# Attention and gated-MLP backward on one core: dK and dV matmuls levelled over the halves of a head, projections spread, copies moved to ScalarE

## Chip, cores and metric

The kernel runs on one core of a Trainium2 chip. The metric is device time in microseconds of one execution, the median over runs. Engines are named as the profile names them: PE (TensorE matmuls), PEld (its weight loads), DVE (VectorE), ACT (ScalarE), POOL (GpSimd), SP (the queue that issues transposing DMAs here).

## The reference

The output and eight gradients of `x + s * silu(B(xn))` are computed, where `xn` is a layer norm of `x`, `s` is an attention block over a given K and V cache, and `B` a gated MLP. Sizes: 2048 tokens, model width 576, 32 heads of width 128, MLP width 4608, bf16.

```python
def _A_ref(x, k_cache, v_cache, wq, wo):            # per head, Dh = 128
    q = (x @ wq).reshape(B, Sq, H, Dh).transpose(0, 2, 1, 3)
    scores = jnp.einsum("bhqd,bhkd->bhqk", q, k_cache) * (Dh ** -0.5)
    p = _softmax(scores, axis=-1)
    o = jnp.einsum("bhqk,bhkd->bhqd", p, v_cache)
    return o.transpose(0, 2, 1, 3).reshape(B, Sq, H * Dh) @ wo
...
_out, _vjp = jax.vjp(_f, A_x, A_k_cache, A_v_cache, A_wq, A_wo, B_w_gate, B_w_up, B_w_down)
return (_out, *_vjp(grad_out))
```

For each head the backward pass needs P = softmax(Q K^T), O = P V, dV = P^T dO, dP = dO V^T, dS = P * (dP - delta) with delta the row sums of O * dO, dQ = dS K and dK = dS^T Q.

## The kernel before

The program has stages one after the other: the MLP forward, a small stage for `silu` and the gradient that enters the attention, then the 32 heads, then the output projection and the gradients of the weights and of `x`. Only the heads are touched here; they take about 470 to 3600 us of the span, and a few microseconds of tail.

**A head.** There are 16 q tiles of 128 rows (`NT`), and each is done in two halves of 1024 key columns. In the first phase `s_half` makes scores: two matmuls of 512 columns into a PSUM tile `sp` (pool `ps_big`, two buffers), then DVE writes `sneg` with a running minimum. `s_exp` on ACT makes `P` of the whole row of 2048 in one instruction, into a slab. In the second phase `dp_half` makes dP in the same two PSUM buffers; either ACT (with the bias `negdelta`, into `t`) and then DVE's multiplication, or DVE alone in one `scalar_tensor_tensor`, makes `dS`, into a slab too. For the q tiles in `STT2` (4, 9, 14) both halves go to DVE alone; for the others the first half goes by ACT. The pool `slab` has 20 buffers for the 16 `P` and 16 `dS` of a head.

O and dQ need `P` and `dS` transposed: `trans_dma` issues a transposing DMA from SP for each row (tiles `PT`, `dST`, 7 buffers); only `dS` of q tile 9 is transposed by TensorE (`PE_DS`, `trans_pe`). `row_mm` then accumulates four q tiles per PSUM bank (`rows`, 16 matmuls of 128 columns per tile), and `o_sink` or `dq_sink` takes the bank. dV and dK need no transpose: `kv_mm` takes 128 x 128 blocks of a slab as weights and accumulates over all 16 q tiles. One call of `kv` makes half of dV or of dK in two banks, with 128 matmuls ordered by q tile, eight for each; its `sink` copies the banks on ACT (`KVE`) and stores them. There are four such calls per head: VA and VB for dV, KA and KB for dK.

Beside these, per head: `prep_wo` transposes a block of Wo, `proj` makes Q^T (for the next head) and dO^T in four chunks of 512 columns with five matmuls each, and `prep_kt`, `prep_vt`, `prep_don`, `prep_qn` transpose K, V, dO^T and Q^T on TensorE, eight blocks per PSUM bank, two banks each, and copy them out. Pool scales dO (`s_scale`) and Q (`prep_qn`) by the softmax's factors. All of these take their PSUM banks from `ps_acc`, four buffers, which `row_mm` and `kv_mm` use too.

**What sets the order.** For PE, DVE and ACT the order of instructions is the order in which they are emitted (`manual_schedule(engines=MAN)`); Pool and SP are ordered by the framework. Every step is entered with a position: `anchor` for the 64 halves of a head (position = half, `s_half` 0 to 31, `dp_half` 32 to 63), `at` for all others. They are sorted by position, and each step is emitted behind the anchors up to its own position. A position is therefore a place between two halves, not a time. Work of a head may lie past 64, which is inside the next head. Before, a call of `kv` spread its 128 matmuls evenly from one position to another:

```python
VA, VB, KA, KB = (22, 38.0), (38.5, 53.5), (58.0, 69.5), (70.5, 82.0)
QP, DO, KVE, PJE, OUE = (41.0, 3.0), (4.0, 2.5), "ss", "sv", "s"
KT_AT, DON_AT, VT_AT, QN_AT = (46.3, 2, "v"), (7.2, 5, "v"), (22.2, 2, "v"), (38.3, 2, "s")
EXP_AT, RINV_AT, PT_AT, DST_AT, AFTER = 2.1, 4.6, 2.7, 2.0, 3.5
...
at(pos + (end - pos) * (qt * n + j) / (NT * n), kv_mm, bx, hs, slabs, rhs, half, qt, j, sink)
```

The letters choose the engine of a copy: "s" is ACT, "v" is DVE. `rows` of P V start at half 12.1 and of dS K at 44.1 (`XO`, `XQ`), two halves per q tile.

Of the kernel before, what the change touches and what calls it, by code (L numbers as in the profile page):

```python
# [95 lines left out]
def kernel(  # L96
# [312 lines left out]
    with tc.tile_pool(name="ld2", bufs=2) as ld2, tc.tile_pool(name="ld1q", bufs=1) as ld1q, \  # L409
# [17 lines left out]
        def at(pos, fn, *args):  # L427
            prog.append((pos, len(prog), fn, args))
# [56 lines left out]
            alt.copy(hs.woT[:, :DL, :], pt[:, :DL, :], eng=eng)  # L485
            alt.copy(hs.woT[P - KL:, DL, :], pt[P - KL:, DL, :], eng=eng)

        def proj(hs, name, c, eng):
            if c == 0:
# [6 lines left out]
            nc.tensor.matmul(acc[:], lhsT=w[:, DL, :], rhs=xnT[:, DL, cs], start=False, stop=True)
# [23 lines left out]
        def prep_qn(hs, g, eng):  # L520
            if g == 0:
                hs.Qn = ld1q.tile([P, NT, P], bf, name="Qn")
                nc.gpsimd.tensor_scalar(hs.rsc[:], hs.rinv_all[:], SCALE, None, op0=ALU.mult)
            pe_transposes(lambda j: hs.QT[:, j * P:(j + 1) * P], hs.Qn, g, eng)
            gs = slice(g * 8, (g + 1) * 8)
            nc.gpsimd.tensor_tensor(hs.Qn[:, gs, :], hs.Qn[:, gs, :], bcast(hs.rsc[:, gs], 8), op=ALU.mult)
# [142 lines left out]
        VA, VB, KA, KB = (22, 38.0), (38.5, 53.5), (58.0, 69.5), (70.5, 82.0)
        QP, DO, KVE, PJE, OUE = (41.0, 3.0), (4.0, 2.5), "ss", "sv", "s"  # L670
        KT_AT, DON_AT, VT_AT, QN_AT = (46.3, 2, "v"), (7.2, 5, "v"), (22.2, 2, "v"), (38.3, 2, "s")
        EXP_AT, RINV_AT, PT_AT, DST_AT, AFTER = 2.1, 4.6, 2.7, 2.0, 3.5
        WO_AT = 50.0
        MAN = {mybir.EngineType.PE, mybir.EngineType.DVE, mybir.EngineType.Activation}
        for h in range(H):
            hs = Head(h)
# [4 lines left out]
            for c in range(NCH):
                at(back(QP[0] + QP[1] * c), proj, hs, "QT", c, PJE[0])
                at(b + DO[0] + DO[1] * c, proj, hs, "dOT", c, PJE[1])
            at(b + DO[0] - 2, prep_wo, hs, "s")
            for g in range(2):
                at(back(KT_AT[0] + KT_AT[1] * g), prep_kt, hs, g, KT_AT[2])
                at(b + DON_AT[0] + DON_AT[1] * g, prep_don, hs, g, DON_AT[2])
                at(b + VT_AT[0] + VT_AT[1] * g, prep_vt, hs, g, VT_AT[2])
                at(b + QN_AT[0] + QN_AT[1] * g, prep_qn, hs, g, QN_AT[2])
            for p in range(NT // 2):  # L690
                at(b + 4 * p + 2 + RINV_AT, s_rinv, hs, p)
                at(b + max(4 * p + 2.1 + RINV_AT, DON_AT[0] + DON_AT[1] * (p // 4) + 0.5), s_scale, hs, p)
            for qt in range(NT):
# [4 lines left out]
                at(p1 + EXP_AT, s_exp, hs, qt)
                if qt in PE_P:
                    for g in range(2):  # L700
                        at(p1 + 5.3 + g, trans_pe, hs.PT, hs.P, qt, "PT", g, "s")
                else:
                    at(p1 + PT_AT, trans_dma, hs.PT, hs.P, qt, "PT")
                if qt in PE_DS:
                    for g in range(2):
                        at(p2 + 4.3 + g, trans_pe, hs.dST, hs.dS, qt, "dST", g, "sv"[g])
                else:
                    at(p2 + DST_AT, trans_dma, hs.dST, hs.dS, qt, "dST")
            for g in range(NG):
                rows(b + 8 * g + XO, 2, 2, hs, hs.PT, "Vn", g, o_sink(hs, g))  # L710
                rows(b + H1 + 8 * g + XQ, 2, 2, hs, hs.dST, "Kn", g, dq_sink(hs, g))
            for half, (pv, pk_) in enumerate(((VA, KA), (VB, KB))):
                kv(b + pv[0], b + pv[1], hs, hs.P, "dOn", half, out_3[0, h])
                kv(b + pk_[0], b + pk_[1], hs, hs.dS, "Qn", half, out_2[0, h])
# [350 lines left out]
```

## Time and profile before

| | us |
|---|---|
| median of 3 runs (lowest, highest) | 5124.49 (5123.4, 5145.9) |
| span of the profiled execution, first to last instruction | 5130.2 |
| time of the profiled execution itself | not given apart |
| busy: PE, PEld | 4970.7, 3593.9 |
| busy: DVE, ACT, POOL | 3252.2, 2268.8, 1473.0 |
| mean granted TensorE clock | 0.996 |

The profile lists the instructions of one execution by engine. A group is named by its line, engine and operation, the tile it writes and the tiles it reads. The end of a matmul is modelled (a matmul of 128 columns is given 219 ns although the next can start 56 ns after it), so times between starts are the better measure on PE. A wait of an engine is put down to the instruction that released the semaphore last.

### The profile page before, as it was taken

The numbers are of one execution on the slowest core, as the hardware profiler recorded it, in microseconds if no ns is written. First come the engines' busy times: TensorE is split into PE (matmuls) and PEld (weight loads), VectorE is DVE, ScalarE is ACT, GpSimd is POOL, SyncE is SP. The second block draws the span as 40 slices with busy tenths as digits, with TensorE's granted clock in tenths as the row PEclk, the third lists the DMA queues.
The fourth block names the chain that finished last, engine by engine and source line by source line (L and its number), as shares of the span: only waits on it lengthen the run. The fifth ranks groups of instructions, "written<-read, shape, count | busy, mean of one in ns | idle before, by whom it ended". The sixth has DMA issues, their size and how long they took to land.

```text
span 5130.2 us, 127328 instructions
## 1 busy us (share of the span) xinstructions
PE 4970.7 (97%) x54403; PEld 3593.9 (70%) x55312; DVE 3252.2 (63%) x5077; ACT 2268.8 (44%) x2875; POOL 1473.0 (29%) x2165
## 2 busy tenths in 40 slices
PE   9998999999999999999999999999899999999999
PEld 3344777777777777777777777777757777754554
DVE  6546888888888888888888888878633222210101
ACT  5523655655665566556556655655402222100000
POOL 4322323332333233223323332332222333211000
PEclk9999999999999999999999999999999999999999
DMA  7886999999999999999999999999998776697775
GB/s 261 266 216 153 193 198 201 194 199 199 195 193 200 199 193 201 199 196 197 194 202 198 199 199 199 190 188 198 208 200 240 205 202 192 207 244 158 154 153 119
DMA packets 2712809, 1013.48 MB, mean 198 GB/s; under 512 B 2525744, under 2 KB 2648624, under 8 KB 2712240
## 3 DMA queue, kind: packets, MB, share of 16 engines
q1 hardware_dynamic: 2626976, 719.49, 81.3%
q0 software_dynamic: 85264, 285.79, 19.1%
q8 instruction: 432, 7.08, 0.6%
q14 instruction: 137, 1.12, 0.1%
HBM read 172.54 MB, written 201.00 MB: 73 GB/s over the span
## 4 chain that ended last, share of the span: by engine, by line
PE 84%; DVE 6%; issue 5%; DMA 4%; POOL 1%; SPq 1%; ACT 0%; DVEq 0%; POOLq 0%; ACTq 0%
PE acckv L615 17%; PE acc L596 15%; PE acc L1006 8%; PE dp L566 7%; PE sp L536 5%; PE accw L888 5%; PE accp L495 5%; DVE sneg L538 4%; PE dh L847 3%; PE acc L377 3%; PE accd L865 3%; PE acc L944 2%; PE acct L502 2%; PE acc L794 2%; PE accq L953 2%
## 5 line engine op out<-in xcount | busy, mean ns | idle before, releaser
L547 ACT ACTIVATE Pq<-sneg,nm 128x2048 bf16<-128x2048 bf16 x512 | 1024.5, 2001 | 389.0 <-DVE sneg L538 385.9
L596 PE MATMUL acc<-Kn,dST 128*128 128x128 bf16 x8192 | 1067.8, 219 | 25.9 <-DMA dST<-dSq 24.0
L615 PE MATMUL acckv<-dOn,Pq 128*128 128x128 bf16 x8192 | 1033.4, 219 | 15.2 <-POOL negdelta L650 0.2
L596 PE MATMUL acc<-Vn,PT 128*128 128x128 bf16 x8192 | 1024.4, 219 | 8.8 <-DMA PT<-Pq 7.0
L569 DVE SCALAR_TENSOR_TENSOR dSq<-dp,delta,Pq 128x1024 bf16<-128x1024 f32 x608 | 773.5, 1280 | 350.5 <-PE dp L566 248.2
L615 PE MATMUL acckv<-Qn,dSq 128*128 128x128 bf16 x8192 | 897.5, 220 | 8.4 <-issue 0.2
L615 PEld LDWEIGHTS <-Pq 128*128 128x128 bf16 x8192 | 794.2, 98 | 117.7 <-issue 1.3
L596 PEld LDWEIGHTS <-dST 128*128 128x128 bf16 x8192 | 759.6, 98 | 159.7 <-DMA dST<-dSq 30.4
L596 PEld LDWEIGHTS <-PT 128*128 128x128 bf16 x8192 | 766.9, 98 | 149.2 <-DMA PT<-Pq 9.3
L615 PEld LDWEIGHTS <-dSq 128*128 128x128 bf16 x8192 | 719.7, 98 | 100.1 <-issue 0.8
L538 DVE TENSOR_SCALAR_CACHE_REDUCE sneg<-sp,nm 128x1024 bf16<-128x1024 f32 x512 | 656.4, 1282 | 83.4 <-PE sp L536 45.9
L538 DVE TENSOR_SCALAR_CACHE_REDUCE sneg<-sp 128x1024 bf16<-128x1024 f32 x512 | 624.8, 1220 | 61.8 <-PE sp L536 44.2
L572 ACT ACTIVATE t<-dp,negdelta 128x1024 bf16<-128x1024 f32 x416 | 463.6, 1114 | 423.8 <-PE acc L596 237.9
L536 PE MATMUL sp<-KT,QT 128*128 128x512 bf16 x1764 | 548.6, 380 | 34.3 <-DVE sneg L538 27.5
L566 PE MATMUL dp<-VT,dOT 128*128 128x512 bf16 x1727 | 541.0, 380 | 0.8 <-DVE dSq L569 0.8
L555 POOL TENSOR_TENSOR dOn<-dOn,rinv_all 128x256 bf16<-128x256 bf16 x256 | 155.8, 609 | 659.2 <-DVE rinv_all L551 540.4
L576 DVE TENSOR_TENSOR dSq<-t,Pq 128x1024 bf16<-128x1024 bf16 x416 | 318.9, 767 | 0.0
L1019 DVE SCALAR_TENSOR_TENSOR junk<-dxn,xn_all 128x576 f32<-128x576 f32 x16 | 12.1, 758 | 370.7 <-ACT dxn L1014 370.7
L1006 PEld LDWEIGHTS <-cf 128*128 128x128 bf16 x2304 | 146.1, 98 | 142.5 <-DMA cf<-dg_d 4.7
L888 PEld LDWEIGHTS <-xn_all 128*128 128x128 bf16 x2304 | 224.2, 98 | 27.8
L662 POOL DMA_DIRECT2D dq_d<-dq_n x128 | 98.8, 772 | 477.8 <-DVE dq_n L661 452.1
L280 PEld LDWEIGHTS <-xnT 128*128 128x128 bf16 x1152 | 107.1, 98 | 147.2 <-issue 30.9
(188 smaller groups left out, 6966.0 us busy)
## 6 DMA issues: line engine op xcount, KB each, us to landing
out_dram<-kv POOLq DMA_DIRECT2D x256, 128.0 KB, 5.0
h_d<-h_row POOLq DMA_DIRECT2D x48, 384.0 KB, 2.9
a_d<-a_row POOLq DMA_DIRECT2D x48, 384.0 KB, 3.4
b_d<-b_row POOLq DMA_DIRECT2D x48, 384.0 KB, 4.6
a_blk<-a_d SPq DMA_DIRECT2D x18, 1024.0 KB, 5.8
b_blk<-b_d SPq DMA_DIRECT2D x18, 1024.0 KB, 21.8
du_d<-du_blk POOLq DMA_DIRECT2D x18, 1024.0 KB, 8.4
dg_d<-dg_blk POOLq DMA_DIRECT2D x18, 1024.0 KB, 11.5
```

What stands on the lines that cost most here:

```text
L495: nc.tensor.matmul(acc[:], lhsT=w[:, i, :], rhs=srcT[:, i, cs], start=(i == 0), stop=False)
L536: nc.tensor.matmul(sp[:, c * CH:(c + 1) * CH], lhsT=hs.QT[:, qs], rhs=hs.KT[:, hf * HW_ + c * CH: hf * HW_ + (c + 1) * CH], start=True, st ...
L538: nc.vector.tensor_scalar(sneg[:, hf * HW_:(hf + 1) * HW_], sp[:], -SCALE, None if hf == 0 else nm[:, hf - 1:hf], op0=ALU.mult, op1=ALU.mi ...
L547: nc.scalar.activation(Pq[:], sneg[:], AF.Exp, bias=nm[:, hf:hf + 1], scale=-1.0, accum_out=hs.rs_all[:, qt:qt + 1])
L566: nc.tensor.matmul(dp[:, c * CH:(c + 1) * CH], lhsT=hs.dOT[:, qs], rhs=hs.VT[:, hf * HW_ + c * CH: hf * HW_ + (c + 1) * CH], start=True, s ...
L569: nc.vector.scalar_tensor_tensor(dSq[:, hsl], dp[:], hs.delta[:, qt:qt + 1], Pq[:, hsl], op0=ALU.subtract, op1=ALU.mult)
L572: nc.scalar.activation(t[:], dp[:], AF.Identity, bias=hs.negdelta[:, qt:qt + 1], scale=1.0)
L576: nc.vector.tensor_tensor(dSq[:, hsl], t[:], Pq[:, hsl], op=ALU.mult)
L596: nc.tensor.matmul(bx.acc[:, j, :], lhsT=T[qt][:, kt, :], rhs=getattr(hs, rhs)[:, kt, :], start=(kt == 0), stop=(kt == NT - 1))
L615: nc.tensor.matmul(bx.acc[i][:, jj, :], lhsT=slabs[qt][:, k0:k0 + P], rhs=getattr(hs, rhs)[:, qt, :], start=(qt == 0 and jj == 0), stop=(q ...
L888: nc.tensor.matmul(acc[:kd, :FB], lhsT=xn_all[:, st, d0:d0 + kd], rhs=blk_[:, st, :], start=(st == 0), stop=(st == NT - 1))
L1006: nc.tensor.matmul(accs[sl][j][:, :nn], lhsT=ch[:, kk, sl * P:(sl + 1) * P], rhs=w_[:, n0:n0 + nn], start=(pi == 0 and kk == 0), stop=(las ...
```

## The change

- `kv` no longer spreads its matmuls evenly. Each half gets a load in units of a 128-column matmul: two wide matmuls of 512 columns count four each, the P V or dS K row eight, and transposes and projections are added at their positions. `level` fills the halves from position 23.4 with the 512 dK and dV matmuls of a head up to one common level, found by bisection so that they end by 86.8, with a gap of 0.8 between two calls of `kv`. In VA, after each q tile, the position is raised to at least a bound that follows the exps.
- `proj` is emitted matmul by matmul, 0.4 positions apart; Q^T and dO^T chunks get positions of their own, and so do the transposes of K, V, dO and Q, and those of `dS` of q tile 9.
- The copies of dO^T and of V^T go from DVE to ACT.
- `delta`: Pool folds the product `prod` from 128 to 64 to 32 columns with two additions, and DVE sums 32 columns instead of 128. `AFTER` goes from 3.5 to 4.5.
- `prep_qn` makes `rsc` in two parts, one for each half of the q tiles.

```diff
-        def proj(hs, name, c, eng):
+        def proj(hs, name, c, i, eng):
...
-            for i in range(DL):
-                nc.tensor.matmul(acc[:], lhsT=w[:, i, :], rhs=srcT[:, i, cs], start=(i == 0), stop=False)
-            nc.tensor.matmul(acc[:], lhsT=w[:, DL, :], rhs=xnT[:, DL, cs], start=False, stop=True)
-            alt.copy(getattr(hs, name)[:, cs], acc[:], eng=eng)
+            nc.tensor.matmul(acc[:], lhsT=w[:, i, :], rhs=(srcT if i < DL else xnT)[:, i, cs], start=(i == 0), stop=(i == DL))
+            if i == DL:
+                alt.copy(getattr(hs, name)[:, cs], acc[:], eng=eng)
...
-                nc.gpsimd.tensor_scalar(hs.rsc[:], hs.rinv_all[:], SCALE, None, op0=ALU.mult)
...
+            nc.gpsimd.tensor_scalar(hs.rsc[:, gs], hs.rinv_all[:, gs], SCALE, None, op0=ALU.mult)
...
-                    at(pos + (end - pos) * (qt * n + j) / (NT * n), kv_mm, bx, hs, slabs, rhs, half, qt, j, sink)
+                    at(b + pos[qt * n + j], kv_mm, bx, hs, slabs, rhs, half, qt, j, sink)
...
+                for w in (P // 2, P // 4):
+                    nc.gpsimd.tensor_tensor(bx.prod[:, :, :w], bx.prod[:, :, :w], bx.prod[:, :, w:2 * w], op=ALU.add)
...
-                nc.vector.tensor_reduce(hs.delta[:, gs], prod[:], axis=AX.X, op=ALU.add)
+                nc.vector.tensor_reduce(hs.delta[:, gs], prod[:, :, :P // 4], axis=AX.X, op=ALU.add)
...
+        WOT_AT, DST_PE = 2.0, (6.3, 7.8)
+        QT_AT, DOT_AT = ((39.2, 41.6, 47.2, 53.8), "s"), ((5.6, 8.6, 15.8, 18.2), "s")
+        KT_AT, DON_AT, VT_AT, QN_AT = (45.8, 50.2, "v"), (14.0, 25.4, "v"), (29.6, 31.2, "s"), (34.0, 37.6, "s")
+        PSTEP = 0.4
+        EXP_AT, RINV_AT, PT_AT, DST_AT, AFTER = 2.1, 4.6, 2.7, 2.0, 4.5
+
+        KV0, KV1, GAP = 23.4, 86.8, 0.8
...
+        def level(top):
+            out, pos, n = [], KV0, 2 * KPC * NT
+            while pos < 2 * HEAD - 1 and len(out) < 4 * n:
+                if len(out) % n == 0 and out:
+                    pos += GAP
+                k = int(pos)
+                room = max(top - load_[k], 0.01)
+                step = 1.0 / room
+                out.append(pos)
+                pos = min(pos + step, max(k + 1.0, pos + 1e-6)) if step > k + 1.0 - pos else pos + step
+                if len(out) <= n and len(out) % (2 * KPC) == 0:
+                    pos = max(pos, 4.0 * (len(out) // (4 * KPC)) + 8.0)
+            return out, pos
...
+        VA, VB, KA, KB = (kvpos[2 * KPC * NT * k:2 * KPC * NT * (k + 1)] for k in range(4))
```

With these numbers VA runs from position 23.4 to 37.5, VB from 40.8 to 58.2, KA from 59.1 to 69.9 and KB from 70.8 to 86.7.

More of the change, by code (lines that the diff above doesn't have):

```diff
@@ L486, in prep_wo @@
             alt.copy(hs.woT[P - KL:, DL, :], pt[P - KL:, DL, :], eng=eng)
-        def proj(hs, name, c, eng):
-            if c == 0:
+        def proj(hs, name, c, i, eng):
+            if c == 0 and i == 0:
                 setattr(hs, name, ld1.tile([P, S], bf, name=name))
@@ L492, in proj @@
             cs = slice(c * CH, (c + 1) * CH)
-            acc = ps_acc.tile([P, CH], f32, name="accp", tag="acc")
-            for i in range(DL):
-                nc.tensor.matmul(acc[:], lhsT=w[:, i, :], rhs=srcT[:, i, cs], start=(i == 0), stop=False)
-            nc.tensor.matmul(acc[:], lhsT=w[:, DL, :], rhs=xnT[:, DL, cs], start=False, stop=True)
-            alt.copy(getattr(hs, name)[:, cs], acc[:], eng=eng)
+            if i == 0:
+                hs.acc_ = ps_acc.tile([P, CH], f32, name="accp", tag="acc")
+            acc = hs.acc_
+            nc.tensor.matmul(acc[:], lhsT=w[:, i, :], rhs=(srcT if i < DL else xnT)[:, i, cs], start=(i == 0), stop=(i == DL))
+            if i == DL:
+                alt.copy(getattr(hs, name)[:, cs], acc[:], eng=eng)
         def pe_transposes(src_fn, dst, g, eng):
@@ L618, in kv_mm, with kv @@
                 sink(bx.acc[i], i)
-        def kv(pos, end, hs, slabs, rhs, half, out_dram):
+        def kv(b, pos, hs, slabs, rhs, half, out_dram):
             ov = out_dram.rearrange("(p t) d -> p t d", t=NT)
@@ L668 @@
         XO, XQ = 12.1, 12.1
[L669 to L672, printed above, removed]
+        KVE, OUE = "ss", "s"
+        WOT_AT, DST_PE = 2.0, (6.3, 7.8)
+        QT_AT, DOT_AT = ((39.2, 41.6, 47.2, 53.8), "s"), ((5.6, 8.6, 15.8, 18.2), "s")
@@ new lines @@
+        KT_AT, DON_AT, VT_AT, QN_AT = (45.8, 50.2, "v"), (14.0, 25.4, "v"), (29.6, 31.2, "s"), (34.0, 37.6, "s")
+        PSTEP = 0.4
+        EXP_AT, RINV_AT, PT_AT, DST_AT, AFTER = 2.1, 4.6, 2.7, 2.0, 4.5
+        KV0, KV1, GAP = 23.4, 86.8, 0.8
+        BLK, WIDE = 1.0, CH / P
+        load_ = [2 * WIDE + NT / 2] * (2 * HEAD)
+        for p_ in (WOT_AT,):
+            load_[int(p_)] += DT
+        for ps_, n_ in [((KT_AT + DON_AT + VT_AT + QN_AT), 8), ([H1 + 2 * q_ + d_ for q_ in PE_DS for d_ in DST_PE], 8)]:
+            for p_ in ps_:
+                if not isinstance(p_, str):
+                    load_[int(p_)] += n_ * BLK
@@ new lines @@
+        for p_ in QT_AT[0] + DOT_AT[0]:
+            for i in range(DT):
+                load_[int(p_ + PSTEP * i)] += WIDE
+        for k in range(HEAD):
+            load_[HEAD + k] = load_[k]
+        def level(top):
[11 more added lines that the diff above has]
+            return out, pos
@@ L673 @@
+        lo_, hi_ = 10.0, 60.0
+        for _ in range(60):
+            mid = (lo_ + hi_) / 2
+            o_, e_ = level(mid)
+            if len(o_) < 4 * 2 * KPC * NT or e_ > KV1:
+                lo_ = mid
+            else:
+                hi_ = mid
+        kvpos = level(hi_)[0]
+        assert len(kvpos) == 4 * 2 * KPC * NT
+        VA, VB, KA, KB = (kvpos[2 * KPC * NT * k:2 * KPC * NT * (k + 1)] for k in range(4))
         WO_AT = 50.0
@@ L681 @@
             for c in range(NCH):
-                at(back(QP[0] + QP[1] * c), proj, hs, "QT", c, PJE[0])
-                at(b + DO[0] + DO[1] * c, proj, hs, "dOT", c, PJE[1])
-            at(b + DO[0] - 2, prep_wo, hs, "s")
+                for i in range(DT):
+                    at(back(QT_AT[0][c] + PSTEP * i), proj, hs, "QT", c, i, QT_AT[1])
+                    at(b + DOT_AT[0][c] + PSTEP * i, proj, hs, "dOT", c, i, DOT_AT[1])
+            at(b + WOT_AT, prep_wo, hs, "s")
             for g in range(2):
[L686 to L689, printed above, removed]
+                at(back(KT_AT[g]), prep_kt, hs, g, KT_AT[2])
+                at(b + DON_AT[g], prep_don, hs, g, DON_AT[2])
+                at(b + VT_AT[g], prep_vt, hs, g, VT_AT[2])
+                at(b + QN_AT[g], prep_qn, hs, g, QN_AT[2])
             for p in range(NT // 2):
                 at(b + 4 * p + 2 + RINV_AT, s_rinv, hs, p)
-                at(b + max(4 * p + 2.1 + RINV_AT, DON_AT[0] + DON_AT[1] * (p // 4) + 0.5), s_scale, hs, p)
+                at(b + max(4 * p + 2.1 + RINV_AT, DON_AT[p // 4] + 0.5), s_scale, hs, p)
             for qt in range(NT):
@@ L705 @@
                     for g in range(2):
-                        at(p2 + 4.3 + g, trans_pe, hs.dST, hs.dS, qt, "dST", g, "sv"[g])
+                        at(p2 + DST_PE[g], trans_pe, hs.dST, hs.dS, qt, "dST", g, "sv"[g])
                 else:
@@ L712 @@
             for half, (pv, pk_) in enumerate(((VA, KA), (VB, KB))):
-                kv(b + pv[0], b + pv[1], hs, hs.P, "dOn", half, out_3[0, h])
-                kv(b + pk_[0], b + pk_[1], hs, hs.dS, "Qn", half, out_2[0, h])
+                kv(b, pv, hs, hs.P, "dOn", half, out_3[0, h])
+                kv(b, pk_, hs, hs.dS, "Qn", half, out_2[0, h])
         bl = (H - 1) * HEAD
```

## The prediction

> **What bounds the kernel now.** I read the page first, then the windows, then the matmul rows of one head in the middle (the seventh, 1069.9 to 1170.6 us), then ACT, DVE, Pool and the transposing queue around it. A head has 64 halves, numbered 0 to 63; each begins with the two 512-wide matmuls of an `s_half` (0 to 31) or a `dp_half` (32 to 63).
>
> ```profile
> PE 4970.7 (97%) x54403; PEld 3593.9 (70%) x55312; DVE 3252.2 (63%) x5077; ACT 2268.8 (44%) x2875; POOL 1473.0 (29%) x2165
> L484 PE MATMUL acct<-ident,wo_h x32: 219/219/220, 472.5 to 3599.9; 128*128 128x128 bf16 x32
> ```
>
> The second row is the transpose of Wo, once per head: (3599.9 - 472.5)/31 = 100.9 us per head, so 32 heads are some 3230 of the 5130 us. TensorE is busy 97%, so the question is how much of those 100.9 us it only waits.
>
> ```profile
> 1102.23 0.59 PE L536 MATMUL sp<-KT,QT 128*128 128x512 bf16 x2
> 1102.66 0.61 PE L596 MATMUL acc<-Vn,PT 128*128 128x128 bf16 x8
> 1103.11 0.59 PE L536 MATMUL sp<-KT,QT 128*128 128x512 bf16 x2
> 1103.54 0.61 PE L596 MATMUL acc<-Vn,PT 128*128 128x128 bf16 x8
> 1104.24 0.59 PE L536 MATMUL sp<-KT,QT 128*128 128x512 bf16 x2
> 1104.67 0.61 PE L596 MATMUL acc<-Vn,PT 128*128 128x128 bf16 x8
> 1105.66 0.38 PE L536 MATMUL sp<-KT,QT 128*128 128x512 bf16 x1 [0.38 <-DVE sneg L538]
> ```
>
> Columns: start, length, instruction. Without a wait two wide matmuls take 0.43 us (1102.23 to 1102.66) and eight narrow ones 0.45, so 0.216 and 0.056 each (0.0558 over the 19 from 1101.17 to 1102.23). A head has 168 wide and 1109 narrow ones: 168 x 0.2158 + 1109 x 0.0558 = 98.1 us. So 2.8 us of each head are waiting, 90 us in all (1.7%): that is the most this change can win. The same rows show where: halves 18 to 21 hold 0.88 us of matmuls, but sp begins after 1.13 and 1.42 us in halves 19 and 20 counted from 1103.11 and 1104.24, because DVE needs about 1.2 us for each `sneg` and only two score buffers stand between.
>
> Adding what each start is later than 0.056 or 0.216 after the one before, a head loses: half 12 0.38 (a dO transpose waits for a bank that DVE frees with `dq_n`), halves 20 to 22 0.25 + 0.54 + 0.27, half 27 0.45 (DVE late by `VT`, `delta`, `rinv`), half 41 0.16, half 58 0.09: 2.15 in every head. The other 0.67 is a mean over heads, mostly none and sometimes 4 us:
>
> ```profile
> PE sp L536 <- DVE sneg L538: 18.8, 56, 0.4
> PE acc L596 <- DMA dST<-dSq: 10.4, 9, 4.0
> PE acct L502 <- DVE dq_n L661: 6.2, 28, 0.2
> 1129.98 40.07 SPq L584 DMA_TRANSPOSE dST<-dSq  x12
> ```
>
> The first three rows are TensorE's waits over 28 heads: us in total, times, longest (from modelled ends, so 0.16 short each). The last is the transposing queue: 12 transposes back to back, 3.34 us each, while two halves of matmuls bring a new tile every 3.1 us. It is close to a second bound.
>
> **What the change removes.** dOT's four copies (0.69) and VT's two (0.69) leave DVE, and `delta`'s sum shrinks from 512 to 128 elements per partition; that is (4 + 2) x 0.69 + 4 x about 0.45 = 5.9 us per head off DVE. Halves 0 to 31 become 1.54 to 1.61 us of matmuls (22 and 23: 1.38, 1.33), over DVE's 1.2. So 20 to 22 and 27 lose nothing any more, half 12's transposes move two or more halves behind their copies, and half 41's go to other places. I take all 2.15 as gone. The matmuls themselves cost the same: the same 1277 per head, and rows of narrow and wide ones in any order keep 0.056 and 0.216. The split `rsc` is three more Pool operations like `negdelta` (0.22), hidden by Pool's idle 70%.
>
> **What it puts there.** The order of the built instructions gives the place of each matmul in its half; I followed every wait on ACT and DVE through one head. Durations:
>
> ```profile
> L547 ACT ACTIVATE Pq<-sneg,nm 128x2048 bf16<-128x2048 bf16 x512 | 1024.5, 2001 | 389.0 <-DVE sneg L538 385.9
> L40 ACT CAST kv<-acckv 128x512 bf16<-128x512 f32 x256 | 140.3, 587 | 72.5 <-PE acckv L615 61.6 <-ACT Pq L547 6.8
> L40 ACT CAST QT<-accp 128x512 bf16<-128x512 f32 x128 | 74.9, 585 | 198.2 <-PE accp L496 158.4 <-PE dp L566 39.8
> L569 DVE SCALAR_TENSOR_TENSOR dSq<-dp,delta,Pq 128x1024 bf16<-128x1024 f32 x608 | 773.5, 1280 | 350.5 <-PE dp L566 248.2 <-PE acct L502 73.8 <-remote 26.8
> L40 ACT COPY dST<-acct 128x1024 bf16<-128x1024 bf16 x32 | 32.1, 1003 | 0.0
> ```
>
> From a last matmul's end to ACT's or DVE's start, and back to TensorE, the rows of this head show 0.25 us together.
>
> Half 42, 1.30 us. `P` and `dS` share 20 slabs; with 16 `P` and four `dS` alive, the `dS` of q tile 4 (half 40) waits until VB, the second dV half, has used `P` of tile 0. VB ran from half 38.5 and had done so by 39.4; now it starts at 40.8, since the clamp in `level` also acts after VA's last position. Its eighth matmul starts 1.32 us into half 41 (1.60 long); the subtract-multiply of half 40 is behind it, takes 1.28, and `dp` of half 42 needs its buffer: 1.32 + 0.06 + 0.25 + 1.28 - 1.60 = 1.30.
>
> Half 23, 0.68 us. VA's second accumulator takes the bank of KB, the previous head's last dK half, which now ends in half 22; before, four halves lay between. Its `kv` copy stands on ACT behind the exp of q tile 10. That exp starts 1.96 us after the first `sp` matmul of half 21 (1094.77 to 1096.73 in half 13), is followed 2.00 later by the copy (0.59) and 0.05 to TensorE: 4.60 us, where the matmul comes after 1.55 + 1.38 + 0.99 = 3.92.
>
> Half 20, 0.19 us: the fourth dOT projection ends 0.10 us before half 20, its copy on ACT ends 0.73 into it, and the next P-V group wants that bank at 0.54. Half 57, 0.15 us: `t`, then the dST copy (1.00) in the bank that the second dST group wants. Half 39, 0.13 us: DVE's `dSq<-t,Pq` meets Pool's Qn multiply, as in the head read:
>
> ```profile
> 1132.78 1.80 DVE L576 TENSOR_TENSOR dSq<-t,Pq 128x1024 bf16<-128x1024 bf16 x1
> 1132.11 1.91 POOL L526 TENSOR_TENSOR Qn<-Qn,rsc 128x1024 bf16<-128x1024 bf16 x1
> ```
>
> (1.80 where it is else 0.68.) Together 2.45 us. VT's copies on ACT (nearest row: Qn and dST, 1.0) end before half 33 needs them, by 0.8 us; the chain VT, exp, t, exp, t, Qn that follows just fits, by 0.15.
>
> The transposes: unknown. From a `dS` tile's last write to its first row matmul, tiles 0 to 3 had 15.7 to 17.3 us; by the new half lengths 16.6, 13.9, 13.8, 16.4. Tile 7, the usual loser, had 14.7 and gets 15.5. VB's output transfers (128 KB, 5.0 us to landing) also move from half 53 to 58 and the next wq's from 50 to 55, towards tiles 7 and 8. As the queue stays full, I take 0.85 for the 0.67 of today; bounds 0.3 (tile 7 cured) and 1.4 (tiles 1 to 3 wait too).
>
> New Pool adds (nearest row `prod`, 1.19 for 512 elements): an estimate of 0.65 and 0.35, four times each per head, 4 us on an engine idle 70 of 100 us; they end one to two halves before `delta`'s sum, which AFTER = 4.5 moves back by one half. Cost 0; if that cover goes, DVE waits with `sneg` or `dp` behind it, up to 0.3 a head.
>
> **Sum.** Now 2.15 + 0.67 = 2.82; then 2.45 + 0.85 = 3.30: +0.48 x 32 heads = +15 us. That 194 instead of 189 dK matmuls of the last head run after it, and are missing in the first, moves 0.3 us once. The profiled execution spans 5130.2 us, 6 more than the median of 5124.5, and its own time is not given apart; the difference goes on the median: 5140 us, within 0.5% (26 us, about what a measurement of this kernel can tell from no change).
>
> **Rivals.** *Transposes become the bound* (slower): for it the queue without a gap and 3.34 us; against it the 2 us more that tile 7 gets from half 48 to 57. If each head waits 1.5 us: 3.95 - 2.82 = 1.13, x 32 = +36, 5160 us; it decides above 1.15 us a head. Chance 0.29. *Pool's adds hold DVE* (slower): the Trainium skill, "SBUF — State Buffer", section "SBUF: two separate sides", says that a DVE operation with two SBUF inputs and a GpSimd operation that reads SBUF exclude each other for the whole instruction. By that rule the adds of halves 39 to 46 would each stop a `dSq<-t,Pq`, which the 1.80 us row agrees with, though the same operation beside `prod` kept 0.68. In this kernel that is 1 us twice a head on DVE, of which the KT copy of half 46 has 0.4 to spare: 0.6 a head more, 5159. Chance 0.06. *The cure counts and the new waits do not come* (faster): a copy that ACT takes before the exp, a bank freed elsewhere. With half 42 alone, 0.3 of half 23 and 0.3 for the transposes 1.9 remain: -0.9 x 32 = -29, 5095; without half 42 too, 5054; the floor is 5034. Against it: the order of ACT and the slab's wait stand in the built program. Chance 0.18. *It does not do what it says*: partly so, as halves 35, 38 and 58 hold 0.88, 0.88 and 1.05 us; that is in the sum.
>
> **Numbers.** Forecast within 0.5%: 0.47; slower 0.29 + 0.06 = 0.35; faster 0.18. One sign does not hold most of the chance, so the range takes parts of both: low 5102 (2.1 a head), high 5172 (transposes at 1.4, adds at 0.3, 0.15 more on ACT: 4.3). The likeliest case alone is 5125 to 5150.
>
> **What would show it.** Right: in each head a wait of TensorE's `dp` of half 42 for DVE `dSq` of over 1 us (less in the waits view), `acckv` waiting for ACT `kv` 0.5 to 0.7, no wait of `sp` for `sneg` in halves 20 to 27, Wo's transposes 101.4 us apart. Wrong: no `dp` wait there (slab step), waits of `acc` for `dST` above 1 us a head (transposes), or `dSq<-t,Pq` near 1 us in the mean (Pool). Below 100 us per head the forecast has failed on the fast side.

## The result: slower by 0.8%

| | before | changed |
|---|---|---|
| median, us (runs of the same series) | 5127.1 (4) | 5175.6 (4) |
| span of the profiled execution, us | 5130.2 | 5166.4 |
| Wo's transposes, us apart (31 heads) | 100.88 | 102.04 |
| waiting per head, us (28 heads in the middle) | 2.82 | 4.04 |

The changed kernel takes 1.0078 times the time of the one before, 95% interval 1.0055 to 1.0101; the quotient of the two medians, of four runs each, would be 1.0095. The forecast was 5140, range 5102 to 5172, with the most chance (0.47) on a change within 0.5% and 0.35 on a slower kernel. The direction of the sum was right and its size too small: what came is the slower case, and the median lies 3.6 us above the range (the ratio times the 5124.5 of the forecast gives 5164, inside it). The profiled execution's own time is 5168.2 us, 1.8 above its span.

The 36 us are in the heads: Wo's transposes, once per head, run from 470.8 to 3633.9 us, (3633.9 - 470.8)/31 = 102.04 us per head where it was 100.88; 31 x 1.16 = 36.

```profile
L484 PE MATMUL acct<-ident,wo_h x32: 219/219/219, 470.8 to 3633.9; 128*128 128x128 bf16 x32
```

TensorE's waits over the same 28 heads of the changed kernel are three rows (us in total, times, longest; before, it was `sp` for `sneg`, `acc` for the transposes and `acct` for `dq_n`):

```profile
PE dp L567 <- DVE dSq L570: 54.9, 56, 1.2
PE accp L496 <- DVE KT L42: 13.9, 28, 0.5
PE acckv L616 <- ACT kv L40: 13.8, 28, 0.5
```

All waits forecast as removed are gone: no row for `sneg`, none for `dq_n`. But `dp` waits 56 times, twice in each of 28 heads, where one was forecast, and the row of `KT` was not forecast at all. No row for transposes is left. Adding what each start is later than 0.056 or 0.216 after the one before, the loss by half is the same in all 28 heads to some hundredths:

| half | 20 | 23 | 39 | 42 | 47 | 57 | transposes |
|---|---|---|---|---|---|---|---|
| forecast | 0.19 | 0.68 | 0.13 | 1.30 | 0 | 0.15 | 0.85 |
| measured | 0.18 | 0.66 | 0.07 | 1.31 | **1.63** | 0.15 | 0.00 |

The groups of the page show the third number that moved:

```profile
PE 5014.6 (97%) x55312; PEld 3594.7 (70%) x55312; DVE 3195.5 (62%) x4885; ACT 2386.6 (46%) x3067; POOL 1649.7 (32%) x2453
...
L597 PE MATMUL acc<-Kn,dST 128*128 128x128 bf16 x8192 | 1096.7, 219 | 12.1 <-DMA dST<-dSq 12.1
L616 PE MATMUL acckv<-dOn,Pq 128*128 128x128 bf16 x8192 | 1034.9, 219 | 15.3 <-ACT kv L40 15.3
...
L567 PE MATMUL dp<-VT,dOT 128*128 128x512 bf16 x2048 | 609.3, 379 | 62.7 <-DVE dSq L570 62.6
L537 PE MATMUL sp<-KT,QT 128*128 128x512 bf16 x2048 | 608.9, 379 | 8.3 <-DVE sneg L539 8.1
L577 DVE TENSOR_TENSOR dSq<-t,Pq 128x1024 bf16<-128x1024 bf16 x416 | 432.3, 1039 | 0.0
```

DVE should have become 5.9 us per head lighter (189 us), and is only 57 us lighter. The last row says where part of it went: DVE's multiply `dSq<-t,Pq` has a mean of 1039 ns where it had 767, 113 us more over 416 of them. That is the sign named beforehand for "Pool's adds hold DVE". In each of the 28 heads of the changed kernel the multiply that runs in half 44 takes 2.79 us more than the 0.68 it takes alone, and those in halves 36 and 38 take 1.17 and 0.76 more; the 1.12 more of half 40, in the kernel before, is gone.

The timeline of one head in the middle (the seventh) shows both waits. First the forecast one, half 42: DVE's subtract-multiply of half 40 waits for `acckv` (VB's first q tile, the slab), and `dp` of half 42 waits for it. Columns: start, length, instruction, idle time before it and what ended it.

```profile
1140.57 1.28 DVE L570 SCALAR_TENSOR_TENSOR dSq<-dp,delta,Pq 128x1024 bf16<-128x1024 f32 x1 [1.36 <-PE acckv L616]
1141.90 0.59 PE L567 MATMUL dp<-VT,dOT 128*128 128x512 bf16 x2 [1.15 <-DVE dSq L570]
...
1144.83 1.28 DVE L570 SCALAR_TENSOR_TENSOR dSq<-dp,delta,Pq 128x1024 bf16<-128x1024 f32 x1 [1.60 <-PE acckv L616]
1146.03 3.48 DVE L577 TENSOR_TENSOR dSq<-t,Pq 128x1024 bf16<-128x1024 bf16 x1
1149.44 1.27 DVE L570 SCALAR_TENSOR_TENSOR dSq<-dp,delta,Pq 128x1024 bf16<-128x1024 f32 x1
...
1145.49 0.61 POOL L463 DMA_DIRECT2D Vn<-in_A_v_cache_dram  x1 [2.79 <-PE acc L597]
1146.12 1.17 POOL L645 TENSOR_TENSOR prod<-ou,dOn 128x512 f32<-128x512 bf16 x1
1147.23 1.05 POOL L654 TENSOR_TENSOR o_n<-ou,rinv_all 128x512 bf16<-128x512 bf16 x1
1148.23 0.72 POOL L647 TENSOR_TENSOR prod<-prod 128x256 f32<-128x256 f32 x1
...
1150.77 0.59 PE L567 MATMUL dp<-VT,dOT 128*128 128x512 bf16 x2 [0.82 <-DVE dSq L570]
1151.97 0.38 PE L496 MATMUL accp<-xnT,wq_h 128*128 128x512 bf16 x1 [0.50 <-DVE KT L42]
```

Then the other: the multiply that begins at 1146.03 in half 44 takes 3.48 us, not 0.68. The subtract-multiply ahead of it on DVE (1144.83) had itself waited 1.60 us for `acckv`, that is for the slab of q tile 5, so DVE reaches the multiply late. The multiply begins 0.09 before Pool's `prod`, and ends at 1149.51, 0.56 after Pool's first add ends (1148.95). Pool's three operations leave no gap between them. The subtract-multiply behind it on DVE and the K^T copy come 2.8 us late; `dp` of half 47 waits 0.82 and the Q^T projection after it 0.50, by modelled ends (0.16 short each): 1.63 in starts.

### The profile page after: what moved, and what is told of

Its sections match the earlier page's. It is cut to its first block, busy times and chain, and to the rows that moved or that the text cites. A ratio compares the mean times of both kernels' runs of the same rounds, so it can differ in the third digit from the quotient of the medians.

```text
span 5166.4 us, 128591 instructions
## 1 busy us (share of the span) xinstructions
PE 5014.6 (97%) x55312; PEld 3594.7 (70%) x55312; DVE 3195.5 (62%) x4885; ACT 2386.6 (46%) x3067; POOL 1649.7 (32%) x2453
## 4 chain that ended last, share of the span: by engine, by line
PE 89%; DVE 4%; DMA 4%; issue 2%; SPq 1%; ACT 1%; ACTq 0%; POOL 0%; DVEq 0%; POOLq 0%
PE acckv L616 16%; PE acc L597 16%; PE sp L537 8%; PE acc L1053 8%; PE dp L567 7%; PE accp L496 5%; PE accw L935 5%; PE dh L894 3%; PE acc L377 3%; PE accd L912 3%; PE acct L503 3%; PE g_ps L280 2%; PE acc L991 2%; PE u_ps L280 2%; PE accq L1000 2%
## 5 line engine op out<-in xcount | busy, mean ns | idle before, releaser
L597 PE MATMUL acc<-Kn,dST 128*128 128x128 bf16 x8192 | 1096.7, 219 | 12.1 <-DMA dST<-dSq 12.1
L597 PE MATMUL acc<-Vn,PT 128*128 128x128 bf16 x8192 | 1037.0, 219 | 5.3 <-DMA PT<-Pq 4.8
L616 PE MATMUL acckv<-Qn,dSq 128*128 128x128 bf16 x8192 | 963.7, 219 | 0.0
L616 PEld LDWEIGHTS <-Pq 128*128 128x128 bf16 x8192 | 748.2, 98 | 211.2 <-issue 19.6
L616 PEld LDWEIGHTS <-dSq 128*128 128x128 bf16 x8192 | 739.6, 98 | 182.4
L597 PEld LDWEIGHTS <-PT 128*128 128x128 bf16 x8192 | 724.3, 98 | 122.6 <-DMA PT<-Pq 5.7
L567 PE MATMUL dp<-VT,dOT 128*128 128x512 bf16 x2048 | 609.3, 379 | 62.7 <-DVE dSq L570 62.6
L537 PE MATMUL sp<-KT,QT 128*128 128x512 bf16 x2048 | 608.9, 379 | 8.3 <-DVE sneg L539 8.1
L577 DVE TENSOR_TENSOR dSq<-t,Pq 128x1024 bf16<-128x1024 bf16 x416 | 432.3, 1039 | 0.0
L496 PE MATMUL accp<-xnT,wq_h 128*128 128x512 bf16 x640 | 241.4, 382 | 16.2 <-DVE KT L42 15.4
```

The lines of the kernel that those rows point to most:

```text
L496: nc.tensor.matmul(acc[:], lhsT=w[:, i, :], rhs=(srcT if i < DL else xnT)[:, i, cs], start=(i == 0), stop=(i == DL))
L537: nc.tensor.matmul(sp[:, c * CH:(c + 1) * CH], lhsT=hs.QT[:, qs], rhs=hs.KT[:, hf * HW_ + c * CH: hf * HW_ + (c + 1) * CH], start=True, st ...
L567: nc.tensor.matmul(dp[:, c * CH:(c + 1) * CH], lhsT=hs.dOT[:, qs], rhs=hs.VT[:, hf * HW_ + c * CH: hf * HW_ + (c + 1) * CH], start=True, s ...
L577: nc.vector.tensor_tensor(dSq[:, hsl], t[:], Pq[:, hsl], op=ALU.mult)
L597: nc.tensor.matmul(bx.acc[:, j, :], lhsT=T[qt][:, kt, :], rhs=getattr(hs, rhs)[:, kt, :], start=(kt == 0), stop=(kt == NT - 1))
L616: nc.tensor.matmul(bx.acc[i][:, jj, :], lhsT=slabs[qt][:, k0:k0 + P], rhs=getattr(hs, rhs)[:, qt, :], start=(qt == 0 and jj == 0), stop=(q ...
```

## Experiments

The theory after the result: (a) the wait in half 42 is the slab's; (b) half 47's is Pool holding DVE's multiply, which is reached only because (a) has delayed DVE into `prod`. Rivals: the K^T copy's new place is the cause; the adds alone are the cause; the transposing queue takes back what is won.

The table has the us between Wo's transposes, which is sharper than the span: what lies behind the last of them, and is not touched, is 1525 to 1545 us of the span in these runs. It is of one execution of each kernel. The losses named below stand in nearly every one of its 28 heads in the middle, but the waits for transposes fall on a few heads, and executions of one kernel differ by some 35 us (the twelve of e7: 5119 to 5155), which is 1.1 us a head. Each ratio is against runs of the kernel before in the same series; their medians lie between 5127 and 5140.

| kernel | us per head | span | time as a ratio to before |
|---|---|---|---|
| changed | 102.04 | 5166.4 | 1.0078 (1.0055 to 1.0101) |
| e1_no_pool_adds | 102.74 | 5199.4 | 1.0105 (1.0065 to 1.0144) |
| e2_vb_early | 100.99 | 5143.5 | 1.0012 (0.9992 to 1.0033) |
| e3_before_adds | 100.86 | 5135.4 | 1.0012 (0.9993 to 1.0032) |
| e4_vb_early_ka_gap | 100.98 | 5136.6 | 1.0003 (0.9986 to 1.0020) |
| e5_no_two_input_multiply | 101.50 | 5169.6 | 1.0040 (1.0024 to 1.0057) |
| e6_ends_ahead_of_exp | 101.57 | 5156.8 | 1.0017 (1.0001 to 1.0034) |
| e7_dot_earlier | 101.17 | 5146.8 | 1.0002 (0.9984 to 1.0020) |
| e8_second_dst_on_pe | 102.83 | 5184.1 | 1.0113 (1.0090 to 1.0135) |
| e9_combined | 101.39 | 5145.9 | 1.0014 (0.9997 to 1.0032) |
| e10_recip_earlier | 99.93 | 5101.3 | **0.9943 (0.9922 to 0.9963)** |

**The changed kernel without Pool's adds.**

```diff
-                for w in (P // 2, P // 4):
-                    nc.gpsimd.tensor_tensor(bx.prod[:, :, :w], bx.prod[:, :, :w], bx.prod[:, :, w:2 * w], op=ALU.add)
...
-                nc.vector.tensor_reduce(hs.delta[:, gs], prod[:, :, :P // 4], axis=AX.X, op=ALU.add)
+                nc.vector.tensor_reduce(hs.delta[:, gs], prod[:], axis=AX.X, op=ALU.add)
```

> The changed kernel with delta's sum back on DVE alone (no adds on Pool, DVE sums 512 elements again); placement and copies as changed. Seen in the changed kernel: in every head the subtract-multiply's partner dSq<-t,Pq of half 44 takes 3.47 us instead of 0.68 and half 47 loses 1.63 us. Theory (DVE's two-input multiply is held for as long as Pool's multiplies and adds follow each other: prod 1.17, o_n 1.05, add 0.72): without the add it is held 0.72 less, 2.75 us; half 47 loses 0.9; 32 x 0.72 = 23 us less, a span of 5143 us. Rival 1 (Pool has no part; the KT copy's place after the new position of the transposes is the cause): 1.6 stays, 5166. Rival 2 (the adds are the whole cause): half 47 loses nothing, 32 x 1.63 = 52 less, 5114.

In half 44 it came out as the theory said: where the multiply met `prod` (23 of 28 heads) it took 2.79 us, for 2.75 expected, and half 47 lost 0.95 in the median head, for 0.9. Both rivals fall there. But TensorE lost 0.7 us a head more, which no theory expected (the two ratios alone do not tell the kernels apart): without the adds Pool is earlier with the second half of Qn, and that holds another multiply, the one of half 40, for 3.03 us in 26 of 28 heads. Half 42 loses 2.34 instead of 1.31, half 43 another 0.53. From the tenth head of that kernel:

```profile
1456.64 3.03 DVE L577 TENSOR_TENSOR dSq<-t,Pq 128x1024 bf16<-128x1024 bf16 x1
...
1456.09 1.09 POOL L630 DMA_DIRECT2D out_dram<-kv  x2
1457.20 1.91 POOL L527 TENSOR_TENSOR Qn<-Qn,rsc 128x1024 bf16<-128x1024 bf16 x1
```

The multiply starts 0.56 before Qn's, yet ends (1459.67) 0.56 after it (1459.11). So a hold of this length is not tied to the adds.

**VB early.** The clamp no longer acts behind VA's last position.

```diff
-                if len(out) <= n and len(out) % (2 * KPC) == 0:
+                if len(out) < n and len(out) % (2 * KPC) == 0:
```

> The changed kernel with the clamp in level not acting after VA's last position (< for <=): VB starts at 38.55 instead of 40.8, so P of q tile 0 is used up before dS of q tile 4 wants its slab. Theory (slab wait in half 42, and the collision of half 44 follows from it, since DVE runs 0.45 us late behind that wait): half 42's 1.31 and half 47's 1.63 both go; dSq<-t,Pq is near 0.68 again in half 44; 32 x 2.94 = 94 us less, 5072. Rival 1 (the two waits are independent): only 1.31 goes, 42 less, 5124. Rival 2 (given back: the transposing queue, which had 2.9 us more time behind these waits, makes TensorE wait again by the 0.67 of the kernel before or the 0.85 forecast): 5094 to 5100.

Halves 42 and 47 lose nothing, with Pool's adds in place. In the seventh head the multiply of half 44 starts 0.81 us before `prod`, not 0.09, and takes 0.68. So (a) and the second half of (b) hold, and rival 1 (independent waits) falls. Of the 2.94 us only 1.05 arrived:

```profile
PE accp L496 <- ACT kv L40: 34.3, 29, 1.2
PE acckv L616 <- ACT kv L40: 15.8, 28, 0.6
PE acckv L616 <- ACT dST L40: 7.2, 28, 0.3
```

The calls behind VB moved earlier as well, and lose in new places: half 5 1.39 (dO^T's first projection wants a bank of KA, whose copies now stand behind an exp on ACT), half 57 0.43 (KA wants a bank behind the dST copy). The transposes give 0.2.

**The kernel before with the adds alone.**

```diff
+                for w in (P // 2, P // 4):
+                    nc.gpsimd.tensor_tensor(bx.prod[:, :, :w], bx.prod[:, :, :w], bx.prod[:, :, w:2 * w], op=ALU.add)
...
-                nc.vector.tensor_reduce(hs.delta[:, gs], prod[:], axis=AX.X, op=ALU.add)
+                nc.vector.tensor_reduce(hs.delta[:, gs], prod[:, :, :P // 4], axis=AX.X, op=ALU.add)
```

> The kernel before with one part of the change: Pool's two adds per P-V group, DVE sums 128 elements. Theory (the adds hurt only where they meet a two-input multiply of DVE): in the kernel before, prod of the last group starts after DVE's dSq<-t,Pq of half 44 and the add would end near 73.4 us of the head, 0.3 before the next such multiply; dSq<-t,Pq stays 0.68 but for half 40; no loss, 1.6 us of DVE time less per head, 5125 to 5130. Rival (Pool's adds cost in any order): a loss of 0.7 to 1.6 us a head, 5152 to 5182.

No change in time, as the theory said, but not for its reason. The adds cost there too, at second hand: they make Pool 1.3 us later with Qn's multiply, and DVE's multiply of half 40, held until that is over, takes 3.12 us in the median where it took 1.80. Half 42 loses 0.63 by it. In return the shorter sum of `delta` takes half 27's loss from 0.45 to 0.05. The expectation looked at half 44 and not at half 40.

**VA one half later.**

Beside the clamp:

```diff
-        QT_AT, DOT_AT = ((39.2, 41.6, 47.2, 53.8), "s"), ((5.6, 8.6, 15.8, 18.2), "s")
-        KT_AT, DON_AT, VT_AT, QN_AT = (45.8, 50.2, "v"), (14.0, 25.4, "v"), (29.6, 31.2, "s"), (34.0, 37.6, "s")
+        QT_AT, DOT_AT = ((39.2, 41.6, 47.2, 53.8), "s"), ((5.6, 8.6, 15.8, 17.8), "s")
+        KT_AT, DON_AT, VT_AT, QN_AT = (45.8, 50.2, "v"), (14.0, 23.2, "v"), (29.6, 31.2, "s"), (34.0, 37.6, "s")
...
-        KV0, KV1, GAP = 23.4, 86.8, 0.8
+        KV0, KV1, GAP = 24.4, 86.8, 0.8
```

> As the kernel with VB early, and VA starts at 24.4 instead of 23.4 (so its second accumulator comes one half after KB's copy), dOn's second transposes fill the place (23.2 for 25.4), and the fourth dOT projection comes 0.4 earlier (17.8). Theory: half 23's 0.66 and half 20's 0.18 go; dOn's copy (0.69) on DVE in halves of 1.27 to 1.32 us makes sp wait for sneg by up to 0.3: 32 x 0.54 to 0.84 = 17 to 27 us below the kernel with VB early alone. Rival (the wait for the kv copy follows the bank and only moves): no more than 6 us below it.

Half 23 (0.72) and half 20 went, with no wait for `sneg` in their place; but the fourth projection, 0.4 earlier, waits 0.67 in half 17 for the copy of the third. Nothing was won: the rival was nearer.

```profile
PE accp L496 <- ACT kv L40: 34.3, 29, 1.2
PE accp L496 <- ACT dOT L40: 14.7, 29, 0.5
```

**No two-input multiply in half 44** (the changed kernel, one number).

```diff
-    STT2 = {4, 9, 14}
+    STT2 = {4, 5, 9, 14}
```

> The changed kernel with q tile 5 added to STT2: both of its halves go through DVE's subtract-multiply from PSUM (1.28 us, one SBUF input), so there is no t and no dSq<-t,Pq in half 44, where Pool's prod, o_n and add follow each other. Nothing else moves. Theory (Pool holds DVE's two-input multiply there): half 47's 1.63 us go, half 42's 1.31 stay (1.1 to 1.6, since DVE has 0.6 more to do); 32 x 1.63 = 52 us less, a span of 5114 us. Rival (the KT copy's bank and place, or DVE's sum of work in halves 42 to 47): half 47 keeps 1.6 or loses more, 5166 to 5180.

```profile
1149.19 2.47 DVE L570 SCALAR_TENSOR_TENSOR dSq<-dp,delta,Pq 128x1024 bf16<-128x1024 f32 x2 [1.60 <-PE acckv L616]
...
1150.48 1.17 POOL L645 TENSOR_TENSOR prod<-ou,dOn 128x512 f32<-128x512 bf16 x1
1151.60 1.04 POOL L654 TENSOR_TENSOR o_n<-ou,rinv_all 128x512 bf16<-128x512 bf16 x1
1152.59 0.72 POOL L647 TENSOR_TENSOR prod<-prod 128x256 f32<-128x256 f32 x1
```

(The lines are from the seventh head.) This is the plainest sign of the hold. Pool does the same at the same place, and DVE's subtract-multiply, with one input in PSUM, is not held: the two take 2.47, and the second runs beside `prod`. Half 47 loses nothing, half 42 keeps 1.31. The gain was smaller than expected, since half 44's `dp` waits 1.09 instead. The reason is the slab again: the first of the two subtract-multiplies, q tile 5's in half 42, waits 1.60 us for `acckv` (first row) and frees its `dp` buffer only then, where ACT's copy into `t` needed no slab. The Trainium skill, "SBUF — State Buffer", section "SBUF: two separate sides", says that a DVE operation with two SBUF inputs and a GpSimd operation that reads SBUF shut each other out for a whole instruction, whichever starts first, and that a DVE operation with at most one SBUF input, outside the two-port modes, does not contend. These runs agree: beside the same Pool run the multiply took 3.48 us, and two subtract-multiplies took 2.47. They differ in one point: the multiply is held over three instructions in a row, although its record starts before the first of them.

**Halves that end ahead of an exp.** Against the kernel with VA later; the lines of `QT_AT` and `KT_AT` are cut to what changes:

```diff
-        DST_PE = (6.3, 7.8)      DOT_AT = (5.6, 8.6, 15.8, 17.8)      DON_AT = (14.0, 23.2)
+        DST_PE = (5.6, 7.0)      DOT_AT = (6.8, 9.2, 15.4, 18.0)      DON_AT = (14.0, 22.0)
-        KV0, KV1, GAP = 24.4, 86.8, 0.8
+        KV0, KV1, GAP = 23.0, 86.0, (0.8, 1.0, 1.5)
...
-                    pos += GAP
+                    pos += GAP[len(out) // n - 1]
```

> VB early, and every dK and dV half placed so that it ends before an exp is issued on ACT and its successor's first matmul comes 1.0 to 1.5 halves later (KA ends 67.8 for 68.5, KB 86.0 for 86.5, VA starts 23.0); dOT's projections at 6.8, 9.2, 15.4, 18.0, dST's transposes 0.8 earlier, dOn's second group at 22.0. In the kernel with VB early half 5 loses 1.39 us, half 23 0.72 and half 57 0.49 to banks whose kv or dST copy stands behind an exp on ACT. Theory: these go; halves 3 to 5 are light (1.49, 0.88, 1.32) and DVE has a dq_n there, so sp waits there up to 0.5; the transposes take 0.3 to 0.8; a head of 98.5 to 99.4 us against 100.9, a span of 5060 to 5090. Rival (the waits only move to other banks or to DVE, as they did in the two kernels before): a head of 100.5 or more, 5125 or more.

Halves 5, 17 and 57 lose nothing (0.03 at most), 2.5 us as planned. But the head takes 101.57 us, as the rival had it. Half 9 loses 1.72 instead, by the same cause (dO^T's second projection, the copy of the first behind an exp), half 36 0.41, half 15 0.29, and the transposes come back:

```profile
PE accp L496 <- ACT dOT L40: 43.7, 28, 1.6
PE acc L597 <- DMA dST<-dSq: 21.4, 20, 3.1
```

**Banks or transposes.** First, from the kernel before this one, the first two lines; then the same kernel with the last two as well, a second `dS` tile on TensorE.

```diff
-        DOT_AT = (6.8, 9.2, 15.4, 18.0)      QN_AT = (34.0, 37.6)
+        DOT_AT = (6.2, 8.8, 15.4, 18.0)      QN_AT = (33.2, 37.6)
...
-    PE_DS = {9}
+    PE_DS = {9, 13}
```

> As the kernel whose halves end ahead of an exp, with dOT's first two projections at 6.2 and 8.8 (there 6.8 and 9.2: the second waits 1.72 us for the first one's copy, which stands behind an exp) and Qn's first transposes at 33.2 for 34.0 (half 36 loses 0.41 to Qn's copy). Theory 1 (TensorE's waits for banks are the loss): both go, a quiet head falls from 100.6 to 98.5 to 98.9 us, the mean over 28 heads to 99.5 at most, a span of 5075 to 5095. Theory 2 (the transposing queue is the bound by now: its 31 transposes filled 94.5 us of 102.2 in the changed kernel and 97.3 of 101 to 102 where waits were taken out): quiet heads fall, but heads that wait for dST become as much more, the mean stays at 100.3 to 101.0, 5110 to 5135.

> The same kernel with dS of q tile 13 transposed by TensorE as well (PE_DS of 9 and 13): 16 narrow matmuls more, 0.9 us a head, and 30 transposes in the queue instead of 31, some 3.1 us less. Theory 2 (the transposing queue is the bound): waits for dST fall to 0.2 a head or less, all heads near 99.3 to 99.8, a span of 5070 to 5095. Theory 1 (banks): 0.9 more than the kernel without it, 32 x 0.9 = 29 us longer.

Half 9's loss went, half 36's rose to 0.95 (`t` now stands behind Qn's copy). The quiet heads fell to 99.5 us, but the mean to 101.2 only: 24 waits for `dST` (32.9 us, 1.2 a head) lengthen the other heads by up to 7 us. That is what theory 2 said, though the mean is 0.2 above its 100.3 to 101.0. With 30 transposes in the queue that row falls to 1.8 us. The waits of the two kernels, over the same 28 heads:

```profile
PE acc L597 <- DMA dST<-dSq: 32.9, 24, 4.8
PE dp L567 <- ACT t L573: 20.7, 27, 0.8
```

```profile
PE dp L567 <- DVE dSq L570: 39.4, 24, 1.7
PE acckv L616 <- ACT kv L40: 22.5, 28, 0.8
PE dp L567 <- ACT t L573: 22.2, 28, 0.8
PE acc L597 <- DMA dST<-dSq: 1.8, 2, 1.5
```

The sum of the queue's transposes says it too: they fill 94.5 of 102.2 us in the changed kernel, 97.6 of 101.2 with 31 and the waits removed, 90.7 of 103.0 with 30. The second kernel was slower all the same, 102.83 us a head where theory 2 had 99.3 to 99.8. Its first row is again Pool and DVE: the multiply of half 40 takes about 3.55 us in 24 of 28 heads, held until Qn's multiply is over, and 0.68 to 0.97 in the others. Half 4 loses 0.97 to a `kv` copy (second row).

**Together, and one last wait.** From the kernel with two `dS` tiles on TensorE; the last two lines are in the second of these kernels only.

```diff
-    STT2 = {4, 9, 14}
+    STT2 = {1, 3, 4, 9, 14}
...
-        DOT_AT = (6.2, 8.8, 15.4, 18.0)      QN_AT = (33.2, 37.6)      GAP = (0.8, 1.0, 1.5)
+        DOT_AT = (5.2, 8.6, 15.6, 18.0)      QN_AT = (34.0, 37.6)      GAP = (0.8, 1.0, 2.0)
...
-        RINV_AT = 4.6
+        RINV_AT = 3.9
```

> Two dS tiles on TensorE (9 and 13) as in the kernel before this one, which had no waits for dST left but new ones: half 42 1.54 (dSq<-t,Pq of half 40 takes 3.55 us where it meets Pool's Qn multiply), half 4 0.97 (kv copy behind an exp), half 36 0.95 (t on ACT behind Qn's copy), half 15 0.31. Here q tiles 1 and 3 go through DVE's subtract-multiply from PSUM (STT2 of 1, 3, 4, 9, 14: no two-input multiply in halves 36 and 40, two t fewer on ACT), KB begins 2.0 halves after KA, dOT's first projections stand at 5.2 and 8.6, Qn's at 34.0. Theory: all four go but for 0.3, floor 99.03 with the 16 narrow matmuls more; 99.3 to 99.9 us a head with little spread, a span of 5075 to 5105. Rival (0.6 us more on DVE in each of halves 34 to 37 and 38 to 41 makes dp wait for the subtract-multiply by about 1 us): 100.5 or more, 5120 or more.

> The combined kernel with the reciprocals of the row sums issued at 3.9 instead of 4.6 (RINV_AT). The combined kernel had one wait of weight left: half 36 2.06 us, VA's last q tiles wait for Pool's dOn multiply, which stood behind the 1.9 us Qn multiply since DVE's reciprocal had slipped behind two subtract-multiplies; now the reciprocal comes before them, and Pool does dOn first. Theory: half 36 falls to 0.4 at most; 99.3 to 99.8 us a head, with 0.2 to 0.3 for dST; 32 x 1.7 = 54 us below the combined kernel's 5145.9, a span of 5085 to 5100. Rival (DVE waits for the exp with the earlier reciprocal in other q tiles and sp pays): 100.5 or more, 5120 or more.

The first has one wait of weight, 2.06 us in half 36 in every head: VA's last q tiles wait for Pool's dOn multiply, which stood behind Qn's, since DVE's reciprocal had slipped behind a subtract-multiply. Its expectation missed by that wait. The number is the rival's (100.5 or more), but the rival's wait, `dp` for the subtract-multiply, is only 0.4 us a head. The second issues the reciprocals earlier and has little left:

```profile
PE dp L567 <- DVE dSq L570: 12.0, 29, 0.4
PE acc L597 <- DMA dST<-dSq: 7.3, 7, 3.1
```

```profile
L484 PE MATMUL acct<-ident,wo_h x32: 219/219/219, 470.2 to 3568.0; 128*128 128x128 bf16 x32
```

(3568.0 - 470.2)/31 = 99.93 us a head: half 36 0.57 (0.4 at most was expected), the transposes and the rest some 0.4, on a floor of 99.03 that has 16 narrow matmuls more. It is 0.57% faster than the kernel before (0.9943, interval 0.9922 to 0.9963) and, by the two ratios, some 1.3% faster than the changed one. The span of 5101.3 is 1 above the range expected.

## Why the prediction was off, step by step

- **What the change removes: right.** Halves 12, 21, 22, 27, 41 and 58 lose nothing; `sp` waits for `sneg` nowhere in the 28 heads.
- **The new waits of halves 20, 23, 42 and 57: right**, to 0.02 us each; half 39 0.07 for 0.13. They were followed through the built order with durations of the profile before, and that was enough. The slab's wait is confirmed by e2, where it vanishes with VB's place.
- **"New Pool adds ... Cost 0; ... up to 0.3 a head": the step that failed.** The meeting that it put at nothing cost 1.63 a head, of which e1 puts 0.7 on the adds (half 47 still loses 0.95 without them) and the rest on `prod` and `o_n`. The cover named was Pool's idle time, but the price is not paid on Pool: it is DVE's multiply that is held. In the rival the mechanism and the place (the K^T copy behind half 46) were right and the size was not: it reckoned with two holds of 1 us, one operation each, and got 0.6; what came is one hold of 2.8 us, `prod`, `o_n` and add together, and 1.63. Two more holds, in halves 36 and 38, cost TensorE no more than the 0.07 of half 39. The evidence used against it, the multiply that kept 0.68 beside `prod`, was misread: in the kernel before `prod`, which begins 0.41 us after that multiply, is itself the longer one (1.28 for 1.17), which agrees with the lock acting the other way round. Calling it the "adds'" hold was also too narrow: without them (e1) it only fell to 2.79 there and grew elsewhere. And the step did not ask what the slab's wait, found two paragraphs before, does to DVE's place against Pool: by e2 the collision of half 44 exists only behind that wait.
- **The transposes: 0.85 forecast, 0.00 measured; the term was mis-sized.** That does not mean that the queue has room: the waits of halves 42 and 47 give it 2.9 us per head (how much each of the two relieves it is not shown). Where they are removed it comes back (by the waits view 0.2, 0.4, 0.9 and 1.3 us a head in e2, e4, e6 and e7, with the `PT` tiles). The rival "transposes become the bound" was wrong for this kernel and right for what lies behind it.
- **Sum.** 0.18 + 0.66 + 0.07 + 1.31 + 1.63 + 0.15 = 4.00, for 2.82 before: 1.2 more a head, for 0.48 forecast. The two errors, +1.63 and -0.85, partly cancelled; that the number came as near as it did is luck to that extent.

Left open: which multiplies are held for how long. Those of 3.48, 3.03 and 3.55 us all began while Pool was still issuing a DMA ahead of its multiply, and were held from there on. But the start in such an issue does not decide it. In the kernel before, the multiply of half 44 begins 0.05 us into the issue of `Vn`, the one in which the multiply of 3.48 began, and takes 0.68 in all 28 heads; and in the seventh head of the kernel with the 3.55, where it began 0.05 us into an issue of `out_dram` as it did in the others, it took 0.68 too. The records of Pool do not tell these apart, so a model of the lock good enough to forecast each meeting is not to be had from these runs.

## What to carry to other kernels

Take DVE instructions with two SBUF inputs and everything that Pool computes as one resource: list both in order of time, and price the hold. In these runs a multiply that begins inside a Pool instruction is held until that one ends; one that begins while Pool issues a DMA ahead of a run without a gap can be held for the whole run. When a new wait is found, carry its delay through the following halves before the next term is priced, since it moves every later meeting of two engines. And when waits are removed from a kernel with a nearly full queue (here its transposes fill 94.5 of 102.2 us), expect the queue to take some back; the kernel that paid here has one transpose fewer in the queue, and was not run without that.

## What was not expected of the hardware

The multiplies of 3.48, 3.03 and 3.55 us (0.68 alone) each ended 0.56 to 0.57 us after the last Pool instruction of a run, wherever they had started. But a run without a gap does not always hold the multiply to its end. In the changed kernel, in the head shown above:

```profile
1133.01 1.85 DVE L577 TENSOR_TENSOR dSq<-t,Pq 128x1024 bf16<-128x1024 bf16 x1
1135.97 1.44 DVE L577 TENSOR_TENSOR dSq<-t,Pq 128x1024 bf16<-128x1024 bf16 x1
...
1132.41 1.90 POOL L527 TENSOR_TENSOR Qn<-Qn,rsc 128x1024 bf16<-128x1024 bf16 x1 [0.67 <-ACT Qn L40]
1134.27 1.60 POOL L645 TENSOR_TENSOR prod<-ou,dOn 128x512 f32<-128x512 bf16 x1
1135.83 1.04 POOL L654 TENSOR_TENSOR o_n<-ou,rinv_all 128x512 bf16<-128x512 bf16 x1
1136.82 1.17 POOL L647 TENSOR_TENSOR prod<-prod 128x256 f32<-128x256 f32 x1
```

These multiplies, of halves 36 and 38, start while a Pool instruction computes (`Qn`, `o_n`), and end 0.55 us after that one (1134.86 for 1134.31, 1137.41 for 1136.87), in all 28 heads. The Pool instruction behind it is then the longer one: `prod` takes 1.60 for 1.17 and the add 1.17 for 0.72, so the hold acts the other way as well.
